# A last feed-forward layer, half of its input product by Strassen's algorithm, with partial sums handed from PSUM bank to PSUM bank

## The chip, the cores and the metric

The kernel runs on one core of one Trainium2 chip. The metric is the device time of one execution in microseconds (us), and each kernel is run several times. The profile is a trace of one of these executions; its span is about 2 us shorter than the device time. In the profile PE is the tensor engine (matmul), PEld its weight load, DVE the vector engine, ACT the scalar engine, POOL the GpSimd engine, and SPq is the queue from which all DMA transfers but one in the DMA view of `before` are issued (the other goes from ACTq).

## The reference

Four layers in a row on 2048 tokens of 512 values: linear attention, feed-forward (FFN), the same attention, the same FFN, each behind a layer norm and with a residual.

```python
def _B_ref(x, w1, w2):                       # the FFN
    h = jnp.einsum("bsd,df->bsf", x, w1)     # 512 -> 1376, "input product"
    h = jnp.maximum(h, 0)
    return jnp.einsum("bsf,fd->bsd", h, w2)  # 1376 -> 512, "output product"

x = A_x
x = x + _A_ref(_layernorm(x, axis=-1), A_wqkv, A_wo)
x = x + _B_ref(_layernorm(x, axis=-1), B_w1, B_w2)
x = x + _A_ref(_layernorm(x, axis=-1), A_wqkv, A_wo)
x = x + _B_ref(_layernorm(x, axis=-1), B_w1, B_w2)   # <- the change is in here
```

## The kernel before

The kernel is a list of operations with declared reads and writes. Two tables, `ORDER` and `BANKS`, found by a search before, say in which order each engine takes its operations and which PSUM bank every partial result gets. An operation marked flexible may run on ACT or DVE; the table says on which. So a change of the operations needs new tables, and with them the order of the *whole* program may change.

Tokens come in 4 chunks of 512. The input product of one chunk takes, for each of the 10 full blocks of 128 hidden columns, four matmuls of 128x512 into one bank (512 input values are four times 128), then a ReLU out of PSUM. The last 96 columns go another way, which the change does not touch.

```python
def mm_group(mk, reads, writes, dur, name):      # every matmul is issued here
    def _emit(e, mk=mk):
        last = None
        for (o, l, r, st, sp, skip) in mk():
            last = e.matmul(o, l, r, start=st, stop=sp, skip_group_check=skip)
        return last
    return g.add(PE, _emit, reads, writes, dur, name=name)

def b_h(t):                                      # input product of chunk t
    for c in ([NFC - 1] + list(range(NFC - 1)) if REM_TOK else range(NFC)):
        M = 128 if c < NFC - 1 else FLAST
        b = alloc_bank()
        # ... (the last 96 columns: cut)
        mm_group(lambda b=b, c=c, M=M: [(psv[0:M, b, :], w1[:, d, 128 * c:128 * c + M], Tb[:, 4 * t:4 * t + 4, d, :],
                                         d == 0, d == 3, False) for d in range(4)], ...)
        u = h_unit(c, t)
        g.add_flex([(ACT, lambda e, M=M, b=b, u=u: e.activation(unit_ap(u, M), psv[0:M, b, :], ACTF.Relu), C_ACT_PSUM),
                    (DVE, ...)], [("ps", b)], [("big", u)], name="hrelu%d_%d" % (t, c))

# steps of an FFN layer: input product of chunk t, then output product of chunk t-1
for t in range(NCH):
    steps.append((t, None, lambda t=t: b_h(t)))
    if t >= 1:
        steps.append((None, ..., lambda t=t: o_step(t - 1)))
```

The output product (`o_step`) uses Strassen's algorithm already. It needs sums of blocks of the hidden values (`row_sums`, on DVE) and adds its seven products into the residual with DVE operations of 128x256.

Of the kernel before, what the change touches and what calls it, by code (L numbers as in the profile page):

```python
# [69 lines left out]
class _Graph:  # L70

    def __init__(self):
        self.ops = []
        self.last_w = {}
        self.readers = {}
        self.tile_ops = {}
        self.ntiles = 0

    def new_tile(self):
        self.ntiles += 1  # L80
        self.tile_ops[self.ntiles] = []
        return self.ntiles
# [34 lines left out]
    def add_flex(self, alts, reads=(), writes=(), name=""):  # L117
# [7 lines left out]
17 0 14 12 15 18 13 1 16 19 2 20 22 3 24 4 21 23 25 5 6 26 27 7 28 8 47 29 40 30 31 32a 48 41 33 49 42 71 50 43 34 35  # L125
51 44 36 52 73 37 45 72 53d 38 74 46a 87 58 39a 81 54 89 88 56 76 83 55 60 82 93 57 61 59 77 75 62 84 78 86 63 115 94
119 98 95 64 79 66a 65d 103 80 68a 90 85 69 108 113 67a 92 114 116 99 117 70 100 135 120 91 105 154 141 104 118 155
121 160 110 122 230 109 158 130 156 136 123 132 124d 131 125d 142 126d 128 138 127d 137 133 148 134 143 161 129 139
157 147 159 96 149 140 144 162 97 163 153 101 145 150 146 171 164 166d 167a 176 102 172 151 165d 183 152 169 168d 189
106 185 107 173 111 170 182 112 184 222 186 191 219 177 187 9 190 174 223 220 10 231 175 179 192 11 195 221 178 180  # L130
193 201 196 181 197 232 203 207 198 202 199 204 213 209 205 208 188 210 214 211 215 194 216 200 217 233 206 234 261
212 262 218 263 224 228 225 229 226 249 237a 264 236a 235d 244 238a 265 251 254 227 246 245 252 266 247 259 270 250
256 269 239 255 260 271 267 240 241 268 315 311 316a 317 312d 313 318a 276 248 314a 253 281 273 242 243 272 257 329
274 282 258 275 283 334 330 278 284 277 344 335 333 331 336 339 345 337a 332d 286 338 340 349 346 319 288 347d 291 320
341 342d 287 289 296 350 351 285 321 290 301 293 279 322 298 323 306 297 280 292 294 324 299 303 378 325 358 302 326
379 355 328 359a 327 364 380 356d 308 362 381 365a 357 382 307 376 363d 348 368 309 377a 295 343 310 393 300 369a 304
305 370 394 388 352 371a 353 395 354 397 374 389 396a 390 403 375d 391a 392 437 404 408 383 438 366 385 407 387 360
439 405 384 406a 398 440 386 361a 372 399 367a 457 441 402 400 373d 401a 442 447 458 409 443 452 475 462 453 477 473
456 478 448 480 449 451 463 493 450a 444 494 479 461 496 454 481 423 466 464 459 465d 455a 445 414 424a 446 484 467
460a 474 419 415a 468 476 417 420d 425 418a 416 410 411 412 469 427 426a 413 470 471 495 497 421 428a 472 429 422a 431  # L140
572 430a 433 432a 435 434a 482 436a 498 483 485 499 488 486 500 489 487 504 490 501 505 491 521 502 492 506 526 507
503 508 509 531 510 527 547 511 522 530 536 512 548a 532 513 525 570 549 550 535 571 552 551a 514 556 515d 516a 573
518a 554 519 517d 553a 558 537 555a 520 533 557a 538 534d 560 559a 539d 523 528 540 562 524d 542 529d 561a 564 563d
541 543 566 544 565a 545 546 574 567a 575 577 576 568 578 579 569a 581 580 714 582 590 583 591 715 584 585 592 593 586
595 594 587 597 596 588 618 716 589 598 620 717 601 619 621 623 602 622 629 599 625 624 643 626 600 627 631 603 628
635 604 630 648 605 606 607 644 632 653 608 609 645 633 610 649 636 646 650 647 634 663 638 637 666 664d 655 611 665
613d 670 667a 612d 654 668 671d 615a 616 639 672 669a 640 614d 674 641 673a 617 676 675a 651 652 678 677a 656 657 718
679a 719 680 720 682 681a 723 683a 721 724 684 722 729 685a 725 730 792 734 735 793 737 736 726 738 794 731 739 741
740 727 742 732 728 796 743 733 797 795 745 744 658 798 746 801 660 799 659 802 747 807 800 748 686 749 750 751 693
808 688 661 752 753 687 803 662 754 689 694 804 690 695 691 812 805 813 806 755 815 814 757a 809 817 816 756a 810 819  # L150
818 758a 820 760 759d 811 823 821 642 761 824 822 696 825 697 692 826 698 699 827 828 700 829 830 831 832 706 702 701
707 703 833 834d 835a 713 704 709 836d 838 708 762 705 768 764 710 763 837d 769 711 839 765 712 775 771 770 846 766
772 767 776 847 848 783 778 773 849 777 782 774 785 784 840 850 779 791 786 842 787 841 780 852 843 781 858 853 854
844 905 860 788 859 845 906 861 888 855 789 907 851 862 889 790 890 857 891 863 856 908 892 866 867 909 864 868 895
865 896 873 897 871d 872a 870d 878 869a 898 875 899 893 879 876 880 900 894 874 883 902 910 881 885 901 884 904 947
945 912 915 886 946a 903 948a 951 913 949 877 952a 920 950d 911 887 963 917 882 914 922 968 964 921 916 923 973 969
967 965 970 978 966a 974 971d 977 935 975 979 983 976a 953 980 930 981d 954 924 984 936 918 925 919 955 985 937 1012
956 927 957 940 1013 928 938 926 958 939 932 992 959 931 960 998 993a 933 1014 962 1010 999a 934 1015 942 1008 1016
1011a 996 943 1009a 961 941 929 1006 997a 944 972 1027 1007a 1032 1028 982 1071 986 1031 1033 1017 1037 1072 1019 1018
1022 1073 1038 1000 1023 1041 1039 994 1074 1001a 1075 1040a 1004 1029 1020 1030a 989 987 1021 988 1005a 1002 995d  # L160
990a 1026 1034 991 1035d 1076 1003a 1024 1096 1044 1109 1036 1043 1081 1025a 1107 1086 1077 1042 1078 1091 1087 1114
1082 1090 1128 1108 1085 1111 1110 1112 1125 1083 1092 1084a 1126 1093 1088 1095 1079 1051 1089a 1094d 1059 1080 1052a
1101 1045 1046 1048 1113 1060a 1047 1115 1053 1049a 1097 1050 1055 1098 1100 1099d 1127 1054a 1061 1103 1056a 1102
1104 1105 1129 1106 1057 1062a 1065 1058d 1191 1063 1066a 1067 1064d 1069 1068a 1116 1070a 1118 1117 1189 1121 1130
1190 1119 1122 1132 1131 1120 1123 1135 1124 1133 1136 1145 1134 1137 1140 1146 1138 1149 1150 1141 1139 1155 1142
1144 1151 1166 1143a 1156 1169 1147 1167a 1157 1152 1158d 1154 1148d 1168 1171 1170a 1153d 1192 1159 1173 1160 1172a
1162 1175 1174d 1163 1161 1177 1164 1176a 1165 1181 1178a 1179 1182a 1183 1180a 1193 1184a 1194 1185 1195 1196 1186a
1198 1197 1187 1199 1200 1188a 1203 1245 1201 1204 1210 1202 1207 1246 1208 1247 1205 1222 1209 1225 1223a 1206 1224
1212 1211 1226a 1214 1248 1215 1213 1235 1216 1217 1236a 1227 1218 1219 1229 1228a 1220 1221 1231 1230a 1233 1232a
1237 1234a 1249 1238a 1239 1250 1240a 1241 1251 1252 1242a 1243 1253 1254 1244a 1256 1255 1278 1259 1263 1260 1279  # L170
1264 1257 1265 1266 1258 1268 1267 1261 1282 1269 1262 1283 1280 1296 1284 1270 1281 1297 1273 1298 1271 1274 1301
1272 1287 1302 1299 1288 1275 1285 1276 1292 1286 1277 1303 1300 1293 1289 1304 1294 1305 1295 1290 1306 1310 1314
1291 1307 1315 1311 1313 1308 1312 1309
"""
BANKS = ("0154332452076167067067706067010071667161607170706760607066070711126446526524617063017652340157642017"
         "5324534620117060707106176160167706110716710066761070671061176607071001116677070006746627242647110675"
         "031264750361274531602475167035316420765134")


def _replay(ops, tile_ops, vbank, order_s, banks_s):  # L180
# [12 lines left out]
    for pos, w in enumerate(table):  # L193
# [4 lines left out]
        for v in allocs.get(o.idx, ()):  # L198
            pv = bank_prev.get(vbank[v])
            if pv is not None:  # L200
                assert left[pv] == 0
                for d in tile_ops[pv]:
                    if d.eng == PE and o.eng == PE and not d.dma:
                        o.odeps.append(d)
                    elif d not in o.sdeps:
                        o.sdeps.append(d)
            bank_prev[vbank[v]] = v
# [16 lines left out]
def build_kernel(nc, A_x, A_wqkv, A_wo, B_w1, B_w2, out, n_layers_pairs=2, Q_LATE=3, O_PE_CHUNKS=3, PHI_PATH=3,  # L224
# [17 lines left out]
    with es:  # L242
# [72 lines left out]
        def alloc_bank():  # L315
            return g.new_tile()

        class _PS:

            def __getitem__(self, key):  # L320
                key = list(key)
                key[1] = vbank[key[1]]
                return ps[tuple(key)]
        psv = _PS()

        scr_state = {"e": 0, "sq": 0, "ln": 0, "rem": 0, "sum": 0}

        def dma(emit, reads, writes, xfer_ns, name, eng=SP, issue=C_SP_ISSUE):
            sem = es.enter_context(nc.semaphore("dsem%d" % len(dma_sems)))
# [754 lines left out]
```

## Time and profile before

| | before |
|---|---|
| time, median of 4 runs | 280.11 us (279.92 to 280.26) |
| span of the profiled run | 277.9 us |
| PE busy | 273.7 us, 98% |
| DVE, ACT busy | 80%, 63% of the span |
| chain that ended last | PE 96% |
| PE idle before the first, after the last matmul | 1.24 us, 2.78 us |

The first two lines that matter stand on the page of the profile: the busy time of each engine with the count of instructions, and the make-up of the chain of work that ended last.

```profile
...
PE 273.7 (98%) x1804; PEld 154.4 (56%) x1804; DVE 221.3 (80%) x568; ACT 176.3 (63%) x366; POOL 33.3 (12%) x43
...
PE 96%; ACT 1%; DVE 1%; DVEq 0%; issue 0%
...
```

These are the groups of instructions that the change touches or that stand in for new ones: line, engine, operation, output and inputs, shapes, count, busy us and mean ns of one.

```profile
...
L511 PE MATMUL ps<-Tb,w 128*128 128x512 bf16 x320 | 73.6, 379 | 0.0
L710 ACT ACTIVATE big<-ps 128x512 bf16<-128x512 f32 x70 | 41.3, 596 | 26.6 <-PE ps L511 26.4
...
L495 DVE TENSOR_SCALAR emscr<-escr 128x512 bf16<-128x512 bf16 x64 | 21.2, 338 | 5.2 <-ACT escr L493 4.9
L669 DVE TENSOR_TENSOR big<-big,ps 128x512 bf16<-128x512 bf16 x32 | 20.8, 680 | 0.1
...
L732 DVE TENSOR_TENSOR xin<-big 128x1280 bf16<-128x1280 bf16 x16 | 13.0, 818 | 2.5 <-ACT big L710 2.4
...
```

A matmul's mean of 379 ns covers an overlap with its neighbours and must not be multiplied by the count: 320 x 379 ns are 121 us, where the group is busy for 73.6. The pitch is what counts, and the timeline of PE shows it: 32 matmuls start at 231.09, and the next group starts at 238.00, which is 216 ns each.

```profile
...
231.09 7.07 PE L511 MATMUL ps<-Tb,w 128*128 128x512 bf16 x32
238.00 0.71 PE L511 MATMUL ps<-w2s,big 128*128 128x256 bf16 x5
...
```

The windows show the stage in which the change works. The columns are the stretch, its length, busy us and count for PE, PEld, DVE, ACT and POOL, the granted clock, and DMA.

```profile
...
228.00:234.00 6.00, 6.00 (x42) 3.11 (x41) 5.70 (x19) 4.74 (x12) 0.00 (x0) 1.00 0.34 112
234.00:240.00 6.00, 6.00 (x35) 3.21 (x33) 1.30 (x4) 2.98 (x5) 1.01 (x1) 1.00 0.61 89
240.00:246.00 6.00, 6.00 (x56) 4.93 (x54) 4.10 (x7) 1.19 (x2) 0.00 (x0) 1.00 0.00 0
246.00:252.00 6.00, 6.00 (x53) 4.01 (x50) 4.46 (x9) 2.05 (x4) 0.00 (x0) 1.00 0.12 25
252.00:258.00 6.00, 6.00 (x35) 3.27 (x34) 0.98 (x2) 3.22 (x6) 0.00 (x0) 1.00 0.21 87
...
```

PE is busy throughout. DVE and ACT together have about 29 of 60 engine-us free in these 30 us.

### The profile page before, as it was taken

Reading aid. Unit: us, or ns where it says so; the run is one execution under the profiler, and the core shown is the slowest. Engines: PE = TensorE matmul, PEld = TensorE weight load, DVE = VectorE, ACT = ScalarE, POOL = GpSimd, SP = SyncE. Lnnn points to the kernel's source line nnn. Section 1 sums busy time; section 2 is a strip of 40 time slices with the busy share of each in tenths; the row PEclk is TensorE's granted clock in tenths of the full one; section 3 lists DMA queues with packets and bytes.
Section 4 is the critical chain, followed back from the end, with each engine's and each line's share of the span. In section 5 each row is a group of like instructions: output and inputs, shape, how many; then the busy total and the mean of one; then the engine's idle time right before and its main releaser. Section 6 shows DMA issues by size and latency. Waiting matters only on the chain.

```text
span 277.9 us, 4796 instructions
## 1 busy us (share of the span) xinstructions
PE 273.7 (98%) x1804; PEld 154.4 (56%) x1804; DVE 221.3 (80%) x568; ACT 176.3 (63%) x366; POOL 33.3 (12%) x43
## 2 busy tenths in 40 slices
PE   8999999999999999999999999999999999999995
PEld 3444544444475747655867444433447475675784
DVE  5999659998994895975888887799899597291696
ACT  3988929998566593595167675799886517415200
POOL 3111000001002011041003554000011101000000
PEclk9999999999999999999999999999999999999999
DMA  6945950121222053004003310003023605211004
GB/s 202 382 98 103 287 172 0 36 52 28 57 54 42 2 96 75 2 19 77 2 0 40 75 38 0 2 1 75 4 48 70 73 0 146 27 21 75 0 2 151
DMA packets 41974, 18.32 MB, mean 66 GB/s; under 512 B 36352, under 2 KB 40544, under 8 KB 41952
## 3 DMA queue, kind: packets, MB, share of 16 engines
q1 hardware_dynamic: 41808, 17.96, 27.6%
q8 instruction: 14, 0.23, 0.3%
q10 hardware_dynamic: 144, 0.07, 0.1%
q14 instruction: 8, 0.07, 0.1%
HBM read 7.01 MB, written 2.10 MB: 33 GB/s over the span
## 4 chain that ended last, share of the span: by engine, by line
PE 96%; ACT 1%; DVE 1%; DVEq 0%; issue 0%
PE ps L511 94%; PE ps L395 2%; DVE xn L551 1%; PE ps L474 0%; ACT sqscr L518 0%; DVE xres L524 0%; ACT lden L658 0%; ACT xn L529 0%; ACT lden L660 0%; ACT escr L493 0%; ACT big L491 0%; DVEq L1022 0%; DVE xn L805 0%; DVE wrm L388 0%
## 5 line engine op out<-in xcount | busy, mean ns | idle before, releaser
L511 PE MATMUL ps<-Tb,w 128*128 128x512 bf16 x320 | 73.6, 379 | 0.0
L710 ACT ACTIVATE big<-ps 128x512 bf16<-128x512 f32 x70 | 41.3, 596 | 26.6 <-PE ps L511 26.4
L771 DVE SCALAR_TENSOR_TENSOR xres<-ps,rstdf,xres 128x256 f32<-128x256 f32 x64 | 29.9, 480 | 26.0 <-PE ps L511 25.3
L511 PEld LDWEIGHTS ps<-Tb,w 128*128 128x128 bf16 x320 | 30.7, 98 | 33.5 <-DMA Tb<-xn 0.5
L518 ACT ACTIVATE sqscr<-xres 128x512 bf16<-128x512 f32 x48 | 30.3, 631 | 29.3 <-DVE xres L555 16.1
L493 ACT ACTIVATE escr<-ps 128x512 bf16<-128x512 f32 x64 | 38.1, 618 | 7.4 <-PE ps L511 7.2
L491 ACT ACTIVATE big<-ps 128x512 bf16<-128x512 f32 x64 | 38.5, 623 | 2.2 <-PE ps L511 2.1
L511 PE MATMUL ps<-w,big 128*128 128x256 bf16 (+1 forms) x224 | 34.0, 273 | 0.0
L511 PE MATMUL ps<-big,xn 128*128 128x512 bf16 x128 | 31.0, 379 | 0.0
L497 DVE TENSOR_TENSOR big<-big,emscr 128x512 bf16<-128x512 bf16 x64 | 29.3, 470 | 2.2 <-ACT big L491 1.1
L511 PE MATMUL ps<-wqkv,Tb 128*128 128x512 bf16 x128 | 30.9, 380 | 0.0
L511 PE MATMUL ps<-Tb,wqkv 128*128 128x512 bf16 x128 | 30.8, 379 | 0.1
L511 PE MATMUL ps<-Wp,big 128*128 128x512 bf16 x128 | 30.3, 379 | 0.0
L495 DVE TENSOR_SCALAR emscr<-escr 128x512 bf16<-128x512 bf16 x64 | 21.2, 338 | 5.2 <-ACT escr L493 4.9
L511 PEld LDWEIGHTS ps<-w,big 128*128 128x128 bf16 (+1 forms) x224 | 21.6, 98 | 4.7 <-DVE xres L771 1.0
L544 POOL TENSOR_TENSOR rstdf<-varf,nhalf 128x4 f32<-128x4 f32 x8 | 8.0, 1008 | 127.5 <-DVE varf L542 68.7
L511 PE MATMUL ps<-w,xin 128*128 128x256 bf16 x160 | 22.2, 272 | 0.0
L511 PE MATMUL ps<-w2s,xin 128*128 128x256 bf16 x160 | 22.1, 273 | 0.0
L669 DVE TENSOR_TENSOR big<-big,ps 128x512 bf16<-128x512 bf16 x32 | 20.8, 680 | 0.1
L511 PEld LDWEIGHTS ps<-Tb,wqkv 128*128 128x128 bf16 x128 | 12.1, 98 | 14.5 <-DVE nmf L527 0.5
L511 PEld LDWEIGHTS ps<-Wp,big 128*128 128x128 bf16 x128 | 12.0, 98 | 14.6 <-issue 0.7
L511 PEld LDWEIGHTS ps<-wqkv,Tb 128*128 128x128 bf16 x128 | 12.1, 98 | 14.4 <-ACT Tb L481 1.1
(103 smaller groups left out, 330.5 us busy)
## 6 DMA issues: line engine op xcount, KB each, us to landing
wqkv<-in_A_wqkv_dram SPq DMA_DIRECT2D x3, 512.0 KB, 7.1
xin<-in_A_x_dram SPq DMA_DIRECT2D x3, 512.0 KB, 7.9
out_dram<-xn SPq DMA_DIRECT2D x3, 512.0 KB, 2.6
w<-in_B_w_dram SPq DMA_DIRECT2D x1, 1376.0 KB, 6.7
w<-in_B_w_dram SPq DMA_DIRECT2D x1, 1280.0 KB, 9.8
wo<-in_A_wo_dram SPq DMA_DIRECT2D x1, 512.0 KB, 10.2
Tb<-xn SPq DMA_TRANSPOSE x30, 3.2
xin<-in_A_x_dram SPq DMA_DIRECT2D x1, 384.0 KB, 3.1
```

The costliest lines, as they stand in the source:

```text
L395: last = e.matmul(psv[:, wt, :], wrm[:, 0:128], wrm[:, :], start=True, stop=True)
L491: g.add(ACT, lambda e: e.activation(dst_ap, psv[:, b, :], ACTF.Identity, bias=1.0 + 1e-6, scale=1.0), [("ps", b)], [dst_key], C_ACT_PSUM, ...
L493: g.add(ACT, lambda e: e.activation(escr[:, s, :], psv[:, b, :], ACTF.Exp), [("ps", b)], [("escr", s)], C_ACT_EXP, name=name + "_exp")
L495: g.add(DVE, lambda e: e.tensor_scalar(emscr[:, s, :], escr[:, s, :], 1.0, 1e-6, ALU.min, ALU.add), [("escr", s)], [("emscr", s)], C_DVE_B ...
L497: g.add(DVE, lambda e: e.tensor_tensor(dst_ap, dst_ap, emscr[:, s, :], ALU.max), [dst_key, ("emscr", s)], [dst_key], 340.0, name=name + "_ ...
L511: last = e.matmul(o, l, r, start=st, stop=sp, skip_group_check=skip)
L518: g.add(ACT, lambda e: e.activation(sqscr[:, q, :], xres[:, i, :], ACTF.Square, accum_out=dst[:, i:i + 1]), [("xres", i)], [("sqscr", q), ...
L544: g.add(POOL, lambda e: e.tensor_tensor(rstdf[:, sl], varf[:, sl], nhalf[:, 0:4], ALU.pow), [("varf", t), ("nhalf",)], [("rstdf", t)], C_P ...
L551: g.add(DVE, lambda e: e.scalar_tensor_tensor(xn[:, i, :], psv[:, b, :], rstdf[:, i:i + 1], xres[:, i, :], ALU.mult, ALU.add), rd, [("xn", ...
L669: g.add(DVE, lambda e, j=j: e.tensor_tensor(unit_ap(us[j]), unit_ap(us[j]), psv[:, GB[j], :], ALU.mult), [("big", us[j]), ("ps", GB[j])], ...
L710: g.add_flex([(ACT, lambda e, M=M, b=b, u=u: e.activation(unit_ap(u, M), psv[0:M, b, :], ACTF.Relu), C_ACT_PSUM), (DVE, lambda e, M=M, b=b ...
L771: g.add(DVE, lambda e: e.scalar_tensor_tensor(xres[:, i, cols], psv[:, bank, R], rstdf[:, i:i + 1], xres[:, i, cols], ALU.mult, ALU.add), ...
```

## The change

The intent: in the last FFN, the input product of chunks 2 and 3 over 1280 columns is one 2x2x2 block product (two chunks; two halves of the 512 inputs; column blocks j and j+5). Seven products replace eight. For each of 5 pairs of column blocks that is 7 x 2 = 14 matmuls in place of 16, so 70 in place of 80. The price is four sums of weight blocks, four sums of token blocks, and sums of products. Some of the latter are made by PE itself: a partial sum that is needed twice is copied from its bank to another bank, and PE goes on adding there without the start flag. That is a "seed".

```diff
+        def h_weight_sums():                      # four times, DVE, 128x1280
+            ...
+            tt(0, A21, A22, [])
+            tt(1, A11, W1S[0], [("w1s", 0)])
+            tt(2, A21, A11, [])
+            tt(3, A12, W1S[1], [("w1s", 1)])
+        def b_h_pair(t0, t1):
+            b_h(t0, H_STR + [c + KH for c in H_STR])     # only the last 96 columns
+            b_h(t1, H_STR + [c + KH for c in H_STR])
+            ...                                          # four token sums, DVE, 128x1024
+            def group(jj, j):
+                X, Z = alloc_bank(), alloc_bank()
+                Y1, Y2 = alloc_bank(seeded=True), alloc_bank(seeded=True)
+                ...
+                def prod(name, a, b, bank, first):
+                    (wa, wk_), (tb, tk_) = a, b
+                    mm_group(lambda: [(psv[:, bank, :], wa(c), tb(c), first and c == 0, c == 1, True) for c in range(2)],
+                             wk_ + tk_, [("ps", bank)], 2 * C_MM512, "%s_%d_%d" % (name, t0, j))
+                ...
+                prod("p1", w_raw(0, 0), t_raw(t0, 0), X, True)
+                copy(bank_ap(Y1), bank_ap(X), [("ps", X)], [("ps", Y1)], "c11")      # seed
+                prod("p5", w_sum(0), t_sum(0), Z, True)
+                s5 = f32_slot()
+                copy(lambda: s5[0], bank_ap(Z), [("ps", Z)], s5[1], "c22")
+                prod("p6", w_sum(1), t_sum(1), X, False)
+                s6 = f32_slot()
+                copy(lambda: s6[0], bank_ap(X), [("ps", X)], s6[1], "c12")
+                prod("p3", w_sum(3), t_raw(t1, 1), Z, False)
+                relu_sum(Z, s6, j, t1)                                               # DVE add, then ReLU in SBUF
+                prod("p2", w_raw(0, 1), t_raw(t0, 1), Y1, False)
+                relu(Y1, j, t0)
+                prod("p7", w_sum(2), t_sum(2), X, False)
+                copy(bank_ap(Y2), bank_ap(X), [("ps", X)], [("ps", Y2), ("ps", X)], "c21")   # seed
+                relu_sum(X, s5, KH + j, t1)
+                prod("p4", w_raw(1, 1), t_sum(3), Y2, False)
+                relu(Y2, KH + j, t0)
@@ _replay
+            assert v not in seeded or (pv is not None and pv not in partial)
@@ layer_steps, last layer
+                    steps.append((NCH - 1, None, h_pair))
+                    steps += [(None, None, lambda t=t: o_step(t)) for t in range(NCH - 3, NCH)]
-ORDER = """ ... 1316 entries ... """
+ORDER = """ ... 1369 entries, differing from the first line on ... """
```

(The plumbing that marks banks as partly written, the f32 tiles in old scratch space, and the tables themselves are cut.)

## The prediction

> **What bounds the kernel.** TensorE. On the page of the profile PE is busy 273.7 of 277.9 us (98%) and holds 96% of the chain that ended last. In the windows PE is busy in all of every stretch from 20 to 260 us but for 0.13 us in 180 to 200. PE idles about 1.24 us before the first matmul and 2.9 us after the last. The granted clock is 1.0. DVE is busy 80%, ACT 63%.
>
> **Removed.** In the last FFN, chunks 2 and 3 (512 tokens each) times 1280 columns take 2 x 10 x 4 = 80 matmuls of 128x512. Strassen takes 5 groups x 7 products x 2 = 70. The mean duration shown (379 ns) overlaps the neighbours; the pitch counts: the timeline shows 32 from 231.09 to 238.00, 216 ns each. So 10 x 0.216 = 2.16 us of PE time goes (1804 to 1794 instructions). That is the whole possible gain, 0.77%.
>
> **Added, on DVE and ACT only.** By durations in the groups by form:
> - 20 ReLUs (0.6 us on ACT, 0.69 on DVE) become 10 ReLUs, 20 PSUM copies of 128x512 (0.6 to 0.69), 10 adds of PSUM and an f32 tile (estimate 0.68, like the multiply from PSUM into big) and 10 bf16 ReLUs in SBUF (0.34, like emscr);
> - 4 weight sums of 128x1280 (0.82, like the row sums), 4 token sums of 128x1024 (estimate 0.7).
> Sum 35.0 us against 12.6: about +22 us. In the windows from 228 to 258 us before, DVE is busy 16.5 and ACT 14.2 of 30, so 29 us are free: it fits, but both become 85 to 90% busy there.
>
> **Critical path.** PE never waits if evacuation keeps up. A group is serial: p1, copy, p6 onto the same bank, copy, p7 onto it, copy to a seeded bank, p4, ReLU: about 4 x (0.43 + 0.2 + 0.65), an estimate of 5.1 us, against 3.0 us of PE work. So two groups (8 banks) must be in flight, or other PE work between. The new order does interleave two to three groups, with chunk 1's output product at the end. It also puts nine groups of chunk 1's input product (8 us) between the last attention output and the first product that needs chunk 3's transposed tokens; those take an estimated 6.5 us (residual, centring, two transposes of about 3 us, one token sum). Tight, but in order. I expect PE waits of 0.1 to 0.3 us on copies in the Strassen stage, 0.4 us in all. The order of the whole program was drawn anew: +-0.2 us. The tail stays.
>
> [...] I expect a correct result. No trace of before shows it.
>
> **Prediction.** 280.01 - 2.16 + 0.4 = 278.3 us, range 277.7 to 279.5. Faster by over 2%: 0.01; within 2%: 0.98; slower by over 2%: 0.01.
>
> **What would show it.** PE busy about 271.5 us, 1794 matmuls; PE waits for copies between 235 and 258 us, each below 0.3 us; DVE busy about +13, ACT +9 us, both above 80% in that stage; PE idle at head and tail unchanged.
>
> **What would make it wrong.** The stage becoming bound by ACT and DVE (PE waits of 1 us and more, gain gone); chunk 3's transposes late (one long PE wait before p5); an added op far dearer than its stand-in, such as the f32 add; the new order opening waits elsewhere.

280.01 - 2.16 + 0.4 = 278.25, put as 278.3. The numbers of the chain can be read from the trace of `before`: 0.43 us are two pitches of 216 ns; 0.2 us pass from the end of a block's fourth pitch to the start of its ReLU (for the matmuls from 231.09 us on, blocks end at 236.27 and 237.14 and the ReLUs on ACT start at 236.47 and 237.34); 0.65 us lie between a ReLU of 0.60 us on ACT and one of 0.69 on DVE. A transpose of tokens lands 3.2 us after its issue (DMA view of `before`).

## The result, and the profile after

| | before | after |
|---|---|---|
| time, median | 280.11 us (4 runs, 279.92 to 280.26) | 278.47 us (4 runs, 278.06 to 278.93) |
| ratio | 1 | 0.9942, 95% interval 0.992 to 0.9964 |
| span profiled | 277.9 us | 276.0 us |

Ratios are the mean time of one kernel's runs over that of the other's of the same rounds, so they are not quite the ratio of the medians. Executions over 1.5% slower than the fastest of the same kernel are left out of the means. (The prediction started from 280.01 us, the median of the three runs known then.) The two pages, part 1 and part 4, of the kernel after:

```profile
...
PE 270.5 (98%) x1794; PEld 153.1 (55%) x1794; DVE 237.2 (86%) x600; ACT 178.0 (65%) x372; POOL 34.4 (12%) x43
...
PE 94%; DVE 2%; DMA 2%; ACT 0%; issue 0%; SPq 0%; DVEq 0%
...
```

1794 matmuls, ten fewer, as expected. All that PE waited for, in the waits view (engine, line, waited for: us in total, times, longest):

```profile
...
PE ps L407 <- DVE wrm L400: 1.2, 1, 1.2
PE ps L486 <- DVE xn L967: 0.4, 1, 0.4
PE ps L523 <- DMA Tb<-xn: 0.3, 1, 0.3
PE ps L523 <- ACT Tb L493: 0.3, 1, 0.3
```

The first and second rows belong to the start of the program, the `ACT Tb` row too (at 6.56 us). The `DMA Tb` row is a wait of 0.28 us for a transpose of tokens at 191.50 us, before the first matmul of the last FFN. There is no wait at all for the copies of the Strassen stage. The windows of that stage:

```profile
...
228.00:234.00 6.00, 6.00 (x43) 3.10 (x41) 4.88 (x7) 6.00 (x13) 3.30 (x3) 1.00 0.01 1
234.00:240.00 6.00, 6.00 (x42) 3.06 (x41) 5.58 (x11) 4.62 (x10) 0.00 (x0) 1.00 0.41 46
240.00:246.00 6.00, 6.00 (x35) 3.26 (x34) 5.08 (x12) 3.83 (x7) 0.00 (x0) 1.00 0.00 0
246.00:252.00 6.00, 6.00 (x48) 4.48 (x47) 4.43 (x10) 3.46 (x7) 0.00 (x0) 1.00 0.01 3
252.00:258.00 6.00, 6.00 (x58) 5.35 (x56) 5.94 (x11) 0.00 (x0) 0.00 (x0) 1.00 0.00 0
...
```

PE stays busy throughout. The new work sits on DVE, which is busy 15.1 of 18 us from 234 to 252 and 5.94 of 6 after that; ACT has nothing to do after 252 us (busy 0.00 us from 252 to 274). A piece of the stage in the timeline of PE shows the interleaving. Products can be told apart by their inputs (`escr,wqkv` is p5 or p6, `emscr,wqkv` p7, `emscr,w` p4, `Tb,wqkv` p3, `Tb,w` p1 or p2), and each starts 0.43 us, two pitches of 216 ns, after the one before:

```profile
...
239.36 0.59 PE L523 MATMUL ps<-emscr,w 128*128 128x512 bf16 x2
239.79 0.59 PE L523 MATMUL ps<-escr,wqkv 128*128 128x512 bf16 x2
240.22 0.59 PE L523 MATMUL ps<-Tb,wqkv 128*128 128x512 bf16 x2
240.66 0.59 PE L523 MATMUL ps<-Tb,w 128*128 128x512 bf16 x2
241.09 0.59 PE L523 MATMUL ps<-escr,wqkv 128*128 128x512 bf16 x2
...
```

The added operations as the groups show them. L805 and L806 are the copies, L820 the adds, L822 the ReLUs in SBUF, L756 and L776 weight and token sums:

```profile
...
L805 ACT ACTIVATE ps<-ps 128x512 f32<-128x512 f32 x8 | 4.7, 590 | 0.9 <-PE ps L523 0.5 <-DVE big L820 0.3
...
L820 DVE TENSOR_TENSOR big<-ps,lden 128x512 bf16<-128x512 f32 x6 | 4.0, 687 | 2.1 <-ACT lden L805 1.1 <-ACT ps L805 1.0
...
L822 DVE TENSOR_SCALAR big<-big 128x512 bf16<-128x512 bf16 x10 | 2.6, 287 | 0.0
...
L756 DVE TENSOR_TENSOR wqkv<-w 128x1280 bf16<-128x1280 bf16 x2 | 1.6, 822 | 0.0
...
L776 DVE TENSOR_TENSOR escr<-Tb 128x1024 bf16<-128x1024 bf16 x1 | 0.7, 693 | 0.6 <-DMA Tb<-xn 0.6
...
```

To separate the parts of the program I read three marks from the timelines of every kernel: the second group of transposes on PE (input `ident`, at 7.4 to 8.5 us, where the first loads have come in), the first matmul of the last FFN (`ps<-Tb,w 128*128 128x512`, at 191 to 193 us), and the end of the last matmul. The stretches between them:

| | marks 1 to 2 | last FFN on PE (marks 2 to 3) | mark 3 to end of span |
|---|---|---|---|
| before | 191.58 - 7.78 = 183.80 | 275.12 - 191.58 = 83.54 | 2.78 |
| after | 191.50 - 7.46 = 184.04 | 272.74 - 191.50 = 81.24 | 3.26 |

So the last FFN lost 2.30 us on PE. 10 x 0.216 = 2.16 us of this are the matmuls; the other 0.14 us lies in pauses of at most about 0.2 us between groups of matmuls, which the waits view does not list (counted from the starts and the pitches, they add up to an estimated 0.7 us before and 0.5 us after). The number of matmuls ahead of mark 2 is the same, 1208, in both kernels, so the marks cut the same work. Of these 2.30 us, 0.48 came back after the last matmul, and 0.24 in the first part of the program. The rest of the difference of the spans, 0.32 us, is ahead of mark 1 and is chance at least in part: with the changed kernel's start, mark 1 lies anywhere from 7.46 to 8.52 us in nine profiles, with that of before from 7.43 to 7.87 us in five.

### The profile page after: what moved, and what is told of

Read it like the earlier page. It is cut to its first block, busy times and chain, and to the rows that moved or that the text cites. A ratio compares the mean times of both kernels' runs of the same rounds, so it can differ in the third digit from the quotient of the medians.

```text
span 276.0 us, 4814 instructions
## 1 busy us (share of the span) xinstructions
PE 270.5 (98%) x1794; PEld 153.1 (55%) x1794; DVE 237.2 (86%) x600; ACT 178.0 (65%) x372; POOL 34.4 (12%) x43
## 4 chain that ended last, share of the span: by engine, by line
PE 94%; DVE 2%; DMA 2%; ACT 0%; issue 0%; SPq 0%; DVEq 0%
PE ps L523 93%; DMA xin<-in_A_x_dram 1%; DMA Tb<-xn 1%; DVE xres L536 1%; DVE xn L563 1%; PE ps L486 0%; DVE xn L543 0%; DVE bst L430 0%; ACT Tb L493 0%; DVE nmf L539 0%; SPq L371 0%; DVEq L1155 0%; DVE xn L967 0%; DVE emscr L507 0%; DVE big L509 0%
## 5 line engine op out<-in xcount | busy, mean ns | idle before, releaser
L523 PE MATMUL ps<-Tb,w 128*128 128x512 bf16 x260 | 61.1, 379 | 0.3 <-DMA Tb<-xn 0.3
L523 PEld LDWEIGHTS ps<-Tb,w 128*128 128x128 bf16 x260 | 24.9, 98 | 28.4 <-DMA Tb<-xn 0.6
L503 ACT ACTIVATE big<-ps 128x512 bf16<-128x512 f32 x64 | 37.7, 615 | 3.8 <-PE ps L523 3.6
L724 ACT ACTIVATE big<-ps 128x512 bf16<-128x512 f32 x50 | 28.5, 598 | 9.4 <-PE ps L523 9.4
L523 PE MATMUL ps<-Tb,wqkv 128*128 128x512 bf16 x138 | 33.2, 379 | 0.0
L556 POOL TENSOR_TENSOR rstdf<-varf,nhalf 128x4 f32<-128x4 f32 x8 | 9.1, 1146 | 122.5 <-DVE varf L554 122.5
L507 DVE TENSOR_SCALAR emscr<-escr 128x512 bf16<-128x512 bf16 x64 | 19.4, 317 | 3.1 <-ACT escr L505 2.9
L523 PEld LDWEIGHTS ps<-Tb,wqkv 128*128 128x128 bf16 x138 | 13.2, 98 | 15.5 <-issue 0.5
L523 PEld LDWEIGHTS ps<-wqkv,Tb 128*128 128x128 bf16 x128 | 12.1, 98 | 15.1 <-ACT Tb L493 1.0
```

Of the source, the lines that this page charges most:

```text
L503: g.add(ACT, lambda e: e.activation(dst_ap, psv[:, b, :], ACTF.Identity, bias=1.0 + 1e-6, scale=1.0), [("ps", b)], [dst_key], C_ACT_PSUM, ...
L507: g.add(DVE, lambda e: e.tensor_scalar(emscr[:, s, :], escr[:, s, :], 1.0, 1e-6, ALU.min, ALU.add), [("escr", s)], [("emscr", s)], C_DVE_B ...
L556: g.add(POOL, lambda e: e.tensor_tensor(rstdf[:, sl], varf[:, sl], nhalf[:, 0:4], ALU.pow), [("varf", t), ("nhalf",)], [("rstdf", t)], C_P ...
```

## The experiments

Twelve runs of ten kernels (two kernels ran more than once) were made on three chips; "before" was run beside each. Differences of marks between runs are therefore often between chips; `after_again` on the first chip and `after_third` on the third give the changed kernel there, and the second chip has no run of it. All results are correct except that of `e_bits`.

### The changed kernel once more: `after_again`

No edit.

> The changed kernel once more, unaltered, for a tighter ratio and for a second profile (its four runs fell in two clusters, 278.06 and 278.9 us). Both theories: ratio to before 0.994 +-0.001, PE 1794 matmuls, no PE wait between 226 and 252 us. If the clusters are a matter of the head[...], a profile of a slow execution shows it before 20 us; if of the Strassen stage, PE waits appear between 226 and 252 us.

(The granted clock is 1.00 in the first 10 us of both profiles.)

Measured: 279.11 us (278.38 to 279.37), ratio 0.9967 (0.9953 to 0.9981). The forecast of 0.994 +-0.001 failed. The gain on this chip is about half of the first one, yet marks 2 to 3 are 81.24 us again, and the end 3.24. The loss is ahead of the last FFN. The second statistics operation on DVE, which needs the second load of the input, starts at 5.00 us in place of 4.41, so the first transpose on PE starts at 6.07 in place of 5.47. And marks 1 to 2 take 184.57 us in place of 184.04, with a second wait for a transpose of tokens (0.29 us at 24.67 us) and one of 0.2 us for DVE:

```profile
...
PE ps L523 <- DMA Tb<-xn: 0.6, 2, 0.3
PE ps L486 <- DVE xn L967: 0.4, 1, 0.4
PE ps L523 <- ACT Tb L493: 0.3, 1, 0.3
PE ps L523 <- DVE xres L567: 0.2, 1, 0.2
```

So the 1.2 us between the spans of these two profiles lie in the first 193 us, not in the Strassen stage.

### Order of before for the first part: `e_head` and `e_headtail`

```diff
-ORDER = the change's order
+ORDER = before's up to the first matmul of the last FFN, the change's for all that is left
(e_headtail: and before's again from chunk 3's output product on; BANKS accordingly)
```

> The order and banks of before up to the first matmul of the last FFN (about 191.5 us), those of the changed kernel from there on. Theory 1 (the gain is the 10 matmuls, 2.16 us, and the redrawn order of the first 190 us brings nothing; it costs the PE wait of 0.28 us for a transpose at 191 us): 0.0 to 0.4 us faster than the changed kernel, and no PE wait at 191 us. Theory 2 (a part of the gain comes from the redrawn order of the first 190 us, and the Strassen stage gives less than 2.16): at least 0.4 us slower than the changed kernel.

> As e_head, and the last output product (chunk 3, from about 260 us) in the order of before too. In the changed kernel 3.26 us pass between the end of the last matmul and the end of the span, 2.78 us before. Theory 1 (the tail order lost 0.48 us): 0.3 to 0.5 us faster than e_head. Theory 2 (the tail is bound by DVE, which is 98% busy from 252 us because the Strassen stage pushed chunk 1's and 2's sums and residuals there, so the order does not matter): within 0.2 us of e_head.

Measured: 282.35 and 282.53 us, ratios 1.0088 and 1.0079: slower than both kernels, which neither theory had foreseen. The seam was bad. At that place the two orders have worked off different query blocks, and the ACT operations that the changed order supposes done were not done. In `e_head`, PE waited 2.13 us for them before the first matmul of the last FFN:

```profile
...
193.79 6.18 PE L523 MATMUL ps<-Tb,w 128*128 128x512 bf16 x20 [2.13 <-ACT big L503]
```

The wait cost more than itself. In the three stretches of 2 us after it the granted clock (the third column from the right) was 0.72, 0.50 and 0.93, where it is 1.00 in the changed kernel (windows 194 to 200 us):

```profile
...
194.00:196.00 2.00, 2.00 (x8) 0.83 (x7) 1.96 (x5) 0.60 (x1) 0.00 (x0) 0.72 0.00 0
196.00:198.00 2.00, 2.00 (x6) 0.70 (x5) 0.43 (x1) 1.11 (x2) 0.00 (x0) 0.50 0.00 0
198.00:200.00 2.00, 1.97 (x9) 0.82 (x9) 1.38 (x3) 1.19 (x2) 0.00 (x0) 0.93 0.03 8
...
```

These 20 matmuls took 6.18 us; the same 20 take 4.49 us after the wait of 0.28 us in the changed kernel. So the wait of 2.13 us cost 2.13 + 1.69 = 3.82 us. The drop does not seem to come in every execution: of the twelve executions of `e_head` and `e_headtail`, the two with a mean granted clock of 1.0 took 280.62 and 280.77 us, 1.7 to 1.8 us less than the medians. No run tests what makes the clock drop. `e_head` is inconclusive as a test of the first part. `e_headtail` adds that the old order of the tail is no help: PE waited 0.7 us for a DVE residual there, and the span was 0.3 us longer than that of `e_head`. (After the last matmul it did save 0.41 us, 3.27 in place of 3.68, as its theory 1 had it; but marks 2 to 3 grew by 0.81 us.) As 81.24 and 3.24 us of the changed kernel are to be compared with 82.93 - 1.69 = 81.24 and 3.68 us of `e_head`, nothing is gained in the last FFN either.

### The seam earlier: `e_head2` and `e_head2_again`

```diff
-ORDER = the change's order
+ORDER = before's up to the second attention's key projection, the change's for all that is left
```

> e_head cut the two orders in the middle of an unfinished set of softened queries, and the seam itself made PE wait 2.1 us for ACT; it could not tell the theories apart. Here the seam lies earlier, in the second attention's key projection, where both orders have the same work behind them. Theory 1 (the gain is made in the last FFN; the redrawn order of the first part only costs, by waits of about 0.3 us on transposes at 24 us): as fast as the changed kernel or up to 0.6 us faster, ratio to before 0.991 to 0.995; last FFN (from its first matmul to the end of the span) 84.5 us as in both profiles of the changed kernel, against 86.3 us before. Theory 2 (the redrawn order of the first part brings a part of the gain): ratio above 0.997.

> The kernel of e_head2, unaltered (order of before up to the second attention's key projection, order of the changed kernel after it). Theory 1 (the redrawn first part costs waits on transposes, 0.3 us each): 0.2 to 0.8 us faster than the changed kernel on the same chip. Theory 2 (its lead in the first comparison was the chance of the loads at the start): within 0.2 us.

> The changed kernel, unaltered, on the chip of the next run, for a direct comparison: ratio to before 0.994 to 0.997; last FFN, from its first matmul to the end of its last one, 81.2 us as in its other two profiles (before: 83.5).

Measured: `e_head2` 278.00 us, ratio 0.9925 (0.9903 to 0.9947); `e_head2_again` 278.33 us, ratio 0.9937 (0.9925 to 0.9949). The unaltered changed kernel, `after_third`, took 278.98 us, ratio 0.9965 (0.9951 to 0.9979). On that chip, the mean of the fast runs is 278.31 against 279.04 us, so the mixed order is 0.7 us faster, as theory 1 forecast for this run. This is the best version: it beats both kernels.

Marks 1 to 2 tell where a part of it lies: 191.12 - 7.44 = 183.68 and 191.24 - 7.43 = 183.81 us, like the 183.80 of before; the changed kernel needs 184.04, 184.57 and (`after_third`) 192.22 - 7.93 = 184.29. Marks 2 to 3 are 81.23 and 81.22 us (`after_third`: 81.22), so nothing else in the last FFN differs. The profiles of the direct comparison, whose spans differ by 0.6 us, add up as 0.50 us ahead of mark 1 and 0.48 us from mark 1 to 2, less 0.38 us lost at the end. So the order is shown to shorten marks 1 to 2; but the 0.50 us ahead of mark 1 can be the chance of the first loads, which is theory 2, and without them hardly anything of the lead is left in this pair. One forecast of mine failed: from mark 2 to the end of the span it is 84.88 and 84.86 us, not 84.5. The part after the last matmul takes 3.65 and 3.64 us in place of 3.26, although its instructions and their order are the same. Why is open. The last store lands 1.7 us after its issue in all of these runs (DMA view), so the difference comes after it has landed: from the issue to the end of the span it is 2.4 us in the changed kernel (273.62 to 276.0) and 2.8 us in `e_head2` (273.23 to 276.0). `e_head`, which has the first part of before too, shows a like 3.68 us.

### What bounds the end: `e_hq_act` and `e_hq_dup`

```diff
 e_hq_act, groups 2 to 4:
-g.add(DVE, lambda e: e.tensor_scalar(unit_ap(u), unit_ap(u), 0.0, None, ALU.max), ...)
+g.add(ACT, lambda e: e.activation(unit_ap(u), unit_ap(u), ACTF.Relu), ...)
 e_hq_dup, all groups:
 g.add(DVE, lambda e: e.tensor_scalar(unit_ap(u), unit_ap(u), 0.0, None, ALU.max), ...)
+g.add(DVE, lambda e: e.tensor_scalar(unit_ap(u), unit_ap(u), 0.0, None, ALU.max), ...)   # the same again
```

> The ReLUs in SBUF of groups 2 to 4 (6 of 10) go from DVE to ACT, which is idle from 252 us on; rest as in the changed kernel. Theory 1 (DVE, 98% busy from 252 us to the end, bounds the end of the span: 6 x 0.287 = 1.7 us off DVE let the last store start earlier): last FFN 0.3 to 0.5 us shorter than 84.5 us, gap from the last matmul to the end of the span back from 3.26 to about 2.8 us. Theory 2 (the order of the last residuals makes the longer gap, not the amount of DVE work): no change within 0.1 us.

> Each of the ten ReLUs in SBUF of the Strassen sums is done twice on DVE (same result): 10 x 0.287 = 2.9 us more DVE work in the stage. Theory 1 (DVE bounds the end): last FFN 1.5 to 2.9 us longer than 84.5 us, with PE waits for DVE between 245 us and the end. Theory 2 (PE bounds, DVE has slack): within 0.3 us.

Measured: `e_hq_act` 278.98 us, ratio 0.9947 (0.9928 to 0.9967): marks 2 to 3 81.37 us, end 3.24 us, no change. So the load of DVE does not make the longer end, as theory 2 forecast. Theory 2's own cause, the order, is not tested by this run. What the timelines show at the end is an order of two last residuals: after the last matmul before (end 275.12) DVE ends at 275.74, 0.62 us later; after the change (272.74) at 273.59, 0.85 us later, because a whole tile of 128x512 is dealt with ahead of the last half tile. That is 0.23 of the 0.48 us. For the other 0.25 us, between the issue of the last store and the end of the span, no cause is shown; the DMA view has that store land 1.6 us after its issue before, and 1.7 us after the change.

`e_hq_dup` 280.47 us, ratio 1.0014 (0.9983 to 1.0045): marks 2 to 3 take 82.53 us, 1.29 us more, with waits of PE for DVE:

```profile
...
PE ps L524 <- DVE xres L896: 0.6, 1, 0.6
PE ps L524 <- DMA Tb<-xn: 0.3, 1, 0.3
PE ps L524 <- DVE rhi L807: 0.2, 1, 0.2
```

2.9 us more DVE work cost 1.3 us, between the forecasts of the two theories. An estimate from this: the stage has some 1.6 us of DVE time to spare, and what comes on top goes straight into the time.

### Does the stage count matmuls: `e_three`

```diff
-H_STR=[0, 1, 2, 3, 4]
+H_STR=[0, 1, 2]          # blocks 3, 4, 8, 9 of chunks 2 and 3 by the plain product
```

> Strassen over 3 of the 5 pairs of column blocks, the other two plain (16 matmuls in place of 14 each), at the same places of the order. PE 1798 matmuls, 4 more than the changed kernel, 4 x 0.216 = 0.86 us. DVE and ACT get about 2 x 3.3 + 1.3 + ... = some 8 us less work. Theory 1 (PE counts matmuls in the stage, DVE bounds only the last 0.5 us): last FFN 0.4 to 0.9 us longer than 84.5 us. Theory 2 (DVE's load bounds the stage): shorter or equal, within 0.2 us of 84.5 us.

Measured: 280.16 us, ratio 0.9992 (0.9973 to 1.0012). Marks 2 to 3 take 274.76 - 192.37 = 82.39 us, 1.15 us longer than with five groups, although DVE had 37.8 us of work from 228 to 274 us in place of 41.2 and ACT 15.5 in place of 17.9 (in `after`). 0.86 us are the four matmuls; a wait of about 0.2 us stands in the timeline at 250.93. This is a little over the 0.4 to 0.9 us of theory 1, and opposed to theory 2. Less load on DVE and ACT did not help, more matmuls hurt: with this order the stage is bound by PE.

### One group after the other: `e_seq`

```diff
-PE order in the stage: p5_0 p6_0 p1_1 hr2 p5_1 p7_0 p6_1 p1_2 p3_0 p4_0 p3_1 hr3 p7_1 p2_0 ...   (_0 is group 0)
+PE order in the stage: p1_0 p5_0 p6_0 p3_0 p2_0 p7_0 p4_0 p1_1 p5_1 p6_1 ...
```

ACT and DVE take their work in the order in which it becomes ready. This is a second difference, and the bank table of the stage, redrawn to fit, is a third; neither has a run of its own.

> The five Strassen groups one after the other on PE, each in the order p1 p5 p6 p3 p2 p7 p4, in place of two to three interleaved; ACT and DVE take their work as it becomes ready; rest as in the changed kernel. Theory 1 (the chain of copies from bank to bank is hidden only by interleaving): PE waits of about 0.4 us before p6, 0 to 0.4 before p7 and 0.8 before p4 in each group, 5 to 7 us slower than the changed kernel. Theory 2 (what counts is the throughput of ACT and DVE, which the order does not change): within 1 us of the changed kernel.

Measured: 287.59 us, ratio 1.0277 (1.026 to 1.0293). Marks 2 to 3 take 90.01 us, 8.8 us more. PE waits for copies, in the stage:

```profile
...
PE ps L523 <- ACT ps L805: 4.2, 8, 0.7
PE ps L523 <- DVE ps L806: 1.4, 2, 1.0
...
```

The waits stand where the chain has them: before p6, where the copy of p1 must have been read, and before p4, where the copy into the seeded bank must have been written.

```profile
...
232.58 0.59 PE L523 MATMUL ps<-escr,wqkv 128*128 128x512 bf16 x2
233.41 0.60 PE L523 MATMUL ps<-escr,wqkv 128*128 128x512 bf16 x2 [0.24 <-ACT ps L805]
...
234.79 0.59 PE L523 MATMUL ps<-emscr,wqkv 128*128 128x512 bf16 x2
236.13 0.61 PE L523 MATMUL ps<-emscr,w 128*128 128x512 bf16 x2 [0.75 <-ACT ps L805]
...
```

So the same operations with the same load, in another order, lose four times what the algorithm saves. Theory 1 holds. The copy waits in the view are 5.6 us of the 8.8. The view understates each: it counts from the modelled end of the matmul before. The product ahead of the one at 233.41 started at 232.58, so the next was due two pitches later, at 233.01, and 0.40 us were lost where 0.24 are listed; before the one at 236.13 it is 0.91 us (from 234.79). That fits the 0.4 and 0.8 us forecast. I did not add up the rest, which is waits below what the view lists and waits for DVE. The links of the chain have about the length that the prediction gave them, 0.43 + 0.2 + 0.65 = 1.28 us: from the start of p1 (232.15 in the timeline) to that of p6 (233.41) it is 1.26 us, from p7 (234.79) to p4 (236.13) 1.34 us. After the waits of 0.75 us the granted clock was still 1.00 (windows of `e_seq`, 232 to 238 and 238 to 244 us).

### Without seeds: `e_noseed`

```diff
-copy(bank_ap(Y1), bank_ap(X), [("ps", X)], [("ps", Y1)], "c11")
+copy(lambda: s11[0], bank_ap(X), [("ps", X)], s11[1], "c11")     # to an f32 tile in SBUF
-prod("p2", w_raw(0, 1), t_raw(t0, 1), Y1, False); relu(Y1, j, t0)
+prod("p2", w_raw(0, 1), t_raw(t0, 1), Y1, True);  relu_sum(Y1, s11, j, t0, True)   # DVE add, ACT ReLU
 (the same for c21, p4, Y2)
```

> Strassen without seeds: the two copies that seed a bank for PE (c11, c21) go to f32 tiles in SBUF, PE starts p2 and p4 in fresh banks, and DVE adds the tile when it reads the bank (10 more adds of 0.69 us), ACT does the ReLU in SBUF in place of the one from PSUM. PE work the same as in the changed kernel. Theory 1 (the seeds are what keeps DVE's load within the stage; DVE has about 1.7 us to spare, as the doubled ReLUs showed: 2.9 us more cost 1.2): last FFN 4 to 6 us longer than 84.5 us, with PE waits for DVE from 245 us on. Theory 2 (PE bounds, the seeds are a convenience): within 0.5 us of the changed kernel.

Measured: 282.53 us, ratio 1.0086 (1.0073 to 1.01), slower than before. Marks 2 to 3 take 84.78 us, 3.5 us more than with seeds, a little less than forecast. DVE is busy 43.3 us in 228 to 274 us against 41.2, and PE waits for copies that come late (the tiles `lden`, `rsp` and `escr` are what they are written to):

```profile
...
PE ps L524 <- ACT lden L808: 0.8, 1, 0.8
...
PE ps L524 <- ACT rsp L808: 0.3, 1, 0.3
PE ps L524 <- ACT escr L808: 0.2, 1, 0.2
PE ps L524 <- DVE lden L809: 0.2, 1, 0.2
...
```

The PE work is the same. In this order, Strassen's algorithm without the hand-over from bank to bank makes the kernel slower than the plain product. Whether an order searched for it would do better is open.

### A start over half of a seeded bank: `e_bits`

```diff
+mm_group(lambda: [(psv[:, Y1, 0:256], w_raw(0, 0)[0](0), Tb[:, 4 * t0:4 * t0 + 2, 0, :], True, True, True)],
+         [("w1",)] + T0, [("ps", Y1)], C_MM256, "clr_%d" % j)      # start flag, left half of the bank
 copy(bank_ap(Y1), bank_ap(X), [("ps", X)], [("ps", Y1)], "c11")   # still writes all 512 columns
```

> Wrong on purpose if theory 1 holds. Before each copy that seeds a bank for p2, a matmul with the start flag writes the left 256 of its 512 columns; the copy then overwrites all 512, p2 adds without the start flag. Theory 1[...] the result is wrong. Theory 2 (a matmul without the start flag always adds onto what is in the bank): correct. Time: 5 x 0.11 us more PE work, about 0.5 us, both theories.

Measured: wrong, relative error 0.087, as theory 1 forecast. So theory 2 fails. The copy writes all 512 columns in both kernels; the one difference in the bank is the starting matmul over the left 256 ahead of it. (In the trace one of the five begins at 234.49 us and is modelled to take 0.27 us; the copy is bound to come after it, because both declare the bank as written.) The run does not tell which columns were wrong, nor why. The time of this single look, 280.73 us, holds a wait of 1.1 us for a load at the start and says nothing; marks 2 to 3 are 82.11 us, 0.87 more, of which 0.55 are the five extra matmuls (five of 128x256 take 0.55 us from start to start, 238.00 to 238.55, in the timeline of `before`).

## Why the prediction was right, point by point

The time was right: 278.3 us predicted, 278.47 measured, in the range; so were the two repeats, 279.11 and 278.98 us. That the first result lies so near to the forecast is partly luck: the repeats gained 0.9 to 1.0 us (ratios 0.9967 and 0.9965) where 1.7 us were forecast. The profile of the first comparison also has the smallest loss ahead of the last FFN: marks 1 to 2 take 184.04 us in it, and 184.29 to 184.71 us in the eight other profiles with the same first part.

- *Bound by PE; at most 2.16 us to gain.* Right. Marks 2 to 3 shrank by 2.30 us, and with four matmuls more `e_three` lost 1.15 us of it. PE was busy 270.5 us in place of the 271.5 forecast, because 0.96 us of its waits (0.42 and 0.26 at the start, 0.28 at mark 2) are new.
- *It fits onto DVE and ACT.* Right, but with less to spare than the sum suggested. The added groups sum up to 33.6 us against 35.0 estimated (16 copies on ACT 9.4, 4 on DVE 2.8, 10 ReLUs from PSUM 6.0, adds 6.8, ReLUs in SBUF 2.6, weight sums 3.2, token sums 2.8). The f32 add, which I feared, took 0.69 us, as its stand-in.
- *DVE +13, ACT +9 us, both above 80%.* Wrong in the split: DVE +15.9 (221.3 to 237.2) and ACT +1.7 us (176.3 to 178.0). ACT was busy 11.9 of 18 us from 234 to 252, which is 66%. I had shared out the flexible operations by guess, although the new order table says for each where it goes.
- *A serial chain of 5.1 us for 3.0 us of PE work, hidden by two groups in flight.* Right, as `e_seq` shows by the waits for copies that appear where the chain has them. The forecast for it, 5 to 7 us, was too small: 8.8.
- *Chunk 3's transposes arrive in time.* Right: the second token sum ended at 229.14 + 0.69 = 229.83 us, and the first product that reads one started at 230.66.
- *PE waits of 0.1 to 0.3 us on copies, 0.4 in all.* This step failed. The stage has none. What reduced the gain lies elsewhere: 0.48 us after the last matmul, where I had written that the tail stays, and 0.24 to 0.77 us in the first 190 us (184.04 to 184.57 in the three profiles of the changed kernel against 183.80), where I had allowed 0.2 us either way for the redrawn order. Two sizes were wrong and partly made up for each other: no waits where 0.4 us were expected, and larger losses where almost none were.
- *The seeds give a correct result.* Right: ten seeds in each execution, and all runs of the changed kernel are correct. What is measured is that after a start over half of the bank, ahead of the copy, the result is wrong by 0.087 (`e_bits`). No run tests the assertion in `_replay`, which lets a seed only into a bank whose tile before was a full one.

## What to carry to other kernels

Here PE was busy throughout, and ten matmuls fewer were worth about their pitch (2.30 us in the stage, against 2.16), and only because the sums that pay for them stayed out of PE's way: dropping the seeds cost 3.5 us, and dropping the interleaving of the groups, in the one order tried, 8.8 us. When a change brings a newly searched order of the whole program, take the time between fixed marks, and try the old order on all parts that the change does not touch; here that gave another 0.7 us, of which the marks tie 0.5 us to the order and lose 0.4 us again at the end. Put the seam of two orders where both have the same work behind them: here a PE wait of 2.13 us at the seam cost 3.82 us.
